# Reading alpha by a 128-partition broadcast transfer, and loading the first x chunk in one transfer, in a scaled-residual kernel

## The chip, the cores and the metric

The kernel runs on one core of a Trainium2 chip. A core has five instruction streams: TensorE (PE), VectorE (DVE), ScalarE (ACT), GpSimd (POOL) and SyncE (SP), and sixteen DMA engines that move data between the device memory (HBM) and the on-chip memory (SBUF, 128 partitions). A transfer is issued by an instruction of one stream and is then carried out by the DMA engines beside it.

The metric is the device time of one execution in microseconds (us), lower is better. Three runs of the kernel before gave 162.13, 162.22 and 162.7 us, with a median of 162.22 us.

## The reference

```python
B, S, D = 512, 32, 640
"x": normal (B, S, D) * 0.05, bfloat16
"fx": normal (B, S, D) * 0.05, bfloat16
"alpha": normal (1,) * 0.05 * 0.1, bfloat16

def reference(x, fx, alpha):
    return x + alpha * fx
```

There are 10,485,760 elements in x, as many in fx, and as many in the output, two bytes each. So 41.94 MB have to be read and 20.97 MB written, with one multiplication and one addition for each element, and one scalar that all of them share.

## The kernel before, in words

x, fx and the output are each seen as 128 rows of 81,920 elements, one row for each partition. The columns are cut into five chunks of 16,384 elements (`CHUNK`, line 13; 32 KB for each partition, 4 MB for the whole chunk). For each chunk k there are a load of x (`load_x`, lines 57 to 60), a load of fx (`load_f`, lines 62 to 64), the computation (`compute`, lines 66 to 77: one VectorE instruction that multiplies fx by the scalar and adds x, and writes over the x tile) and a store of that tile (`store`, lines 79 to 84). The last chunk is computed and stored in two halves.

There are four x buffers (`xs`, line 50) and two fx buffers (`fs`, line 51). All loads and stores of the chunks are issued by SP, in an order written out by hand (lines 86 to 106, `manual_schedule` on line 52): x0, fx0, x1, fx1, x2, then fx2, store 0, x3, fx3, store 1, x4, fx4, store 2, store 3, and the two halves of store 4. The transfers share one DMA queue in that order. A load of fx from chunk 2 on waits for the computation that used its buffer two chunks earlier, the load of x4 waits until store 0 has been written out, and each store waits for its computation. The first load alone, x0, is issued as two transfers: partitions 0 to 15, and then partitions 16 to 127 (line 59). The first moves 0.5 MB and the second 3.5 MB.

The scalar alpha is made available on all partitions ahead of everything else (`alpha_to_lanes`, lines 16 to 27). ACT issues a transfer of the single element to partition 0 (line 20); VectorE fills a row of 128 ones (line 22); TensorE multiplies that row by the element, so that every partition receives it (line 24); and VectorE copies the result into a float32 tile `a_f` (line 26), which all the computations read. On VectorE these two small instructions stand ahead of the first computation.

Of the kernel before, what the change touches and what calls it, by code (L numbers as in the profile page):

```python
# [1 line left out]

# [4 lines left out]

ACT = mybir.ActivationFunctionType
ALU = mybir.AluOpType
F32 = mybir.dt.float32  # L10
BF16 = mybir.dt.bfloat16

CHUNK = 16384


def alpha_to_lanes(nc, consts, psum, alpha, eng):

    P = nc.NUM_PARTITIONS
    a_1 = consts.tile([1, 1], alpha.dtype, name="a_1")
    eng.dma_start(out=a_1[:], in_=alpha[None, :])  # L20
    ones = consts.tile([1, P], alpha.dtype, name="ones")
    nc.vector.memset(ones[:], 1.0)  # L22
    a_ps = psum.tile([P, 1], F32, name="a_ps")
    nc.tensor.matmul(a_ps[:], ones[:], a_1[:], start=True, stop=True)  # L24
    a_f = consts.tile([P, 1], F32, name="a_f")
    nc.vector.tensor_copy(out=a_f[:], in_=a_ps[:])  # L26
    return a_f


@with_exitstack  # L30
def kernel(
    ctx: ExitStack,
    tc: tile.TileContext,
    x: bass.AP,
    fx: bass.AP,
    alpha: bass.AP,
    out: bass.AP,
):
    nc = tc.nc
    P = nc.NUM_PARTITIONS  # L40
    xv = x.flatten_outer_dims().rearrange("(p n) d -> p (n d)", p=P)
    fxv = fx.flatten_outer_dims().rearrange("(p n) d -> p (n d)", p=P)
    ov = out.flatten_outer_dims().rearrange("(p n) d -> p (n d)", p=P)
    F = xv.shape[1]
    K = F // CHUNK
    assert K * CHUNK == F and K == 5

    consts = ctx.enter_context(tc.tile_pool(name="consts", bufs=1))
    psum = ctx.enter_context(tc.tile_pool(name="psum", bufs=1, space=bass.MemoryType.PSUM))
    xs = ctx.enter_context(tc.tile_pool(name="xs", bufs=4))  # L50
    fs = ctx.enter_context(tc.tile_pool(name="fs", bufs=2))
    ctx.enter_context(tc.manual_schedule())

    a_f = alpha_to_lanes(nc, consts, psum, alpha, nc.scalar)
    xt, ft = {}, {}

    def load_x(k):
        xt[k] = xs.tile([P, CHUNK], x.dtype, tag="x", name="x_t")
        for a, b in [(0, 16), (16, P)] if k == 0 else [(0, P)]:
            nc.sync.dma_start(out=xt[k][a:b, :], in_=xv[a:b, bass.ts(k, CHUNK)])  # L60

    def load_f(k):
        ft[k] = fs.tile([P, CHUNK], fx.dtype, tag="f", name="f_t")
        nc.sync.dma_start(out=ft[k][:], in_=fxv[:, bass.ts(k, CHUNK)])

    def compute(k, parts=1):
        n = CHUNK // parts
        for j in range(parts):
            s = bass.ts(j, n)
            nc.vector.scalar_tensor_tensor(  # L70
                out=xt[k][:, s],
                in0=ft[k][:, s],
                scalar=a_f[:],
                in1=xt[k][:, s],
                op0=ALU.mult,
                op1=ALU.add,
            )

    def store(k, j=0, parts=1):
        n = CHUNK // parts  # L80
        nc.sync.dma_start(
            out=ov[:, k * CHUNK + j * n : k * CHUNK + (j + 1) * n],
            in_=xt[k][:, bass.ts(j, n)],
        )

    load_x(0)
    load_f(0)
    load_x(1)
    load_f(1)
    load_x(2)  # L90
    compute(0)
    load_f(2)
    store(0)
    load_x(3)
    compute(1)
    load_f(3)
    store(1)
    load_x(4)
    compute(2)
    load_f(4)  # L100
    store(2)
    compute(3)
    store(3)
    compute(4, 2)
    store(4, 0, 2)
    store(4, 1, 2)


# [1 line left out]
_INS = ['x', 'fx', 'alpha']  # L110
_OUTS = [((512, 32, 640), 'bfloat16')]


# [23 lines left out]
```

## Time and profile before

| | us |
|---|---|
| median of three runs | 162.22 |
| the profiled execution: its own time | 162.22 |
| the profiled execution: span from its first to its last instruction | 160.4 |
| VectorE busy | 86.9 |
| of that, the six computations | 86.6 |
| TensorE busy | 0.2 |
| VectorE's waits for a load of fx, five in all | 59.1 |

The profile is of one execution. A page of it gives for each engine its busy time; the span cut into 40 equal slices, with the share of the DMA engines that was busy and the rate at which they moved data; the DMA queues; the chain of work that ended last, followed back from the end; the costliest groups of instructions with what they waited for; and the transfers, with the time from issue to landing, which is when the completion was signalled. The trace behind the page can be asked for any stretch of time, counted from the start of the span. In a view by stretches the rate counts the bytes of a packet at the packet's start. A packet of these transfers is one partition's row of 32 KB (16 KB in the last two stores).

### The profile page before, as it was taken

How to read it: one execution, taken by the hardware profiler on the slowest of the kernel's cores; microseconds unless marked ns; L12 is line 12 of the kernel's file. 1: busy time of each engine (PE TensorE's matmuls, PEld its weight loads, DVE VectorE, ACT ScalarE, POOL GpSimd, SP SyncE). 2: the span in 40 equal slices, each digit the busy share in tenths (PEclk: the TensorE clock that was granted, in tenths of full speed). 3: DMA queues.
4: the chain of work that ended last, by engine and by line, in shares of the span. 5: the costliest groups of instructions: out<-in, count | busy, mean ns of one | idle time of the engine just before them, and what ended most of it. 6: DMA issues, size and time to landing. Idle time of an engine off the chain costs nothing.

```text
span 160.4 us, 88 instructions
## 1 busy us (share of the span) xinstructions
PE 0.2 (0%) x1; PEld 0.1 (0%) x1; DVE 86.9 (54%) x8; POOL 0.2 (0%) x4
## 2 busy tenths in 40 slices
PE   0000000000000000000000000000000000000000
PEld 0000000000000000000000000000000000000000
DVE  0000000099994999949999000999930049998000
POOL 0000000000000000000000000000000000000000
DMA  9799999999999999999999999999999999999991
GB/s 131 139 261 286 253 351 441 449 417 425 449 433 400 457 441 400 441 466 400 433 449 425 425 449 417 408 449 441 417 417 474 392 417 466 417 425 425 400 445 53
DMA packets 2322, 62.92 MB, mean 392 GB/s; under 512 B 274, under 2 KB 274, under 8 KB 274
## 3 DMA queue, kind: packets, MB, share of 16 engines
q1 hardware_dynamic: 2320, 62.92, 97.1%
q10 hardware_dynamic: 2, 0.00, 0.0%
HBM read 41.94 MB, written 20.97 MB: 392 GB/s over the span
## 4 chain that ended last, share of the span: by engine, by line
DMA 59%; DVE 27%; DVEq 5%; SPq 0%; issue 0%
DMA f_t<-in_fx_dram 59%; DVE x_t L70 27%; DVEq L132 5%; SPq L60 0%; DVEq L70 0%
## 5 line engine op out<-in xcount | busy, mean ns | idle before, releaser
L70 DVE SCALAR_TENSOR_TENSOR x_t<-f_t,a_f,x_t 128x16384 bf16<-128x16384 bf16 (+1 forms) x6 | 86.6, 14439 | 59.1 <-DMA f_t<-in_fx_dram 59.1
L26 DVE COPY a_f<-a_ps 128x1 f32<-128x1 f32 x1 | 0.2, 159 | 1.2 <-PE a_ps L24 1.2
L22 DVE MEMSET ones<- 1x128 bf16 x1 | 0.2, 165 | 0.8 <-PEq L121 0.8
L24 PE MATMUL a_ps<-a,ones 1*128 1x1 bf16 x1 | 0.2, 158 | 1.9 <-DMA a<-in_alpha_dram 1.9
L121 POOL MEMSET const-bfloat16-1.0<- 128x1 bf16 x1 | 0.1, 101 | 0.0
L121 POOL MEMSET const-uint8-127<- 128x1 uint8 x1 | 0.1, 101 | 0.0
L121 POOL MEMSET const-float32-0.0<- 128x1 f32 x1 | 0.1, 98 | 0.2 <-issue 0.2
L121 POOL MEMSET const-float32-1.0<- 128x1 f32 x1 | 0.1, 98 | 0.0
L24 PEld LDWEIGHTS <-ones 1*128 1x128 bf16 x1 | 0.1, 97 | 1.0 <-DVE ones L22 1.0
## 6 DMA issues: line engine op xcount, KB each, us to landing
f_t<-in_fx_dram SPq DMA_DIRECT2D x5, 4096.0 KB, 31.3
x_t<-in_x_dram SPq DMA_DIRECT2D x4, 4096.0 KB, 39.8
out_dram<-x_t SPq DMA_DIRECT2D x4, 4096.0 KB, 40.7
out_dram<-x_t SPq DMA_DIRECT2D x2, 2048.0 KB, 11.5
x_t<-in_x_dram SPq DMA_DIRECT2D x1, 3584.0 KB, 21.3
x_t<-in_x_dram SPq DMA_DIRECT2D x1, 512.0 KB, 7.2
a<-in_alpha_dram ACTq DMA_DIRECT2D x1, 0.0 KB
```

Of the source, the lines that this page charges most:

```text
L22: nc.vector.memset(ones[:], 1.0)
L24: nc.tensor.matmul(a_ps[:], ones[:], a_1[:], start=True, stop=True)
L26: nc.vector.tensor_copy(out=a_f[:], in_=a_ps[:])
L70: nc.vector.scalar_tensor_tensor(out=xt[k][:, s], in0=ft[k][:, s], scalar=a_f[:], in1=xt[k][:, s], op0=ALU.mult, op1=ALU.add,)
L121: nc = _bacc.Bacc("TRN2", target_bir_lowering=False, num_devices=1)
L132: with _tile.TileContext(nc) as tc:
```

## The change

The scalar's path loses the ones, the matmul and the PSUM tile. ACT issues instead one transfer whose source is the single element repeated 128 times and whose destination is one bf16 element on each of the 128 partitions. VectorE's copy to float32 stays; it reads that tile in place of the PSUM tile, and so waits for the transfer in place of the matmul. The first load of x is issued as one transfer of 128 partitions, as the other loads are. Nothing else differs: buffers, order and computations are the same.

```diff
-def alpha_to_lanes(nc, consts, psum, alpha, eng):
+def alpha_to_lanes(nc, consts, alpha, eng):
     P = nc.NUM_PARTITIONS
-    a_1 = consts.tile([1, 1], alpha.dtype, name="a_1")
-    eng.dma_start(out=a_1[:], in_=alpha[None, :])
-    ones = consts.tile([1, P], alpha.dtype, name="ones")
-    nc.vector.memset(ones[:], 1.0)
-    a_ps = psum.tile([P, 1], F32, name="a_ps")
-    nc.tensor.matmul(a_ps[:], ones[:], a_1[:], start=True, stop=True)
+    a_b = consts.tile([P, 1], alpha.dtype, name="a_b")
+    eng.dma_start(out=a_b[:], in_=alpha.to_broadcast((P, 1)))
     a_f = consts.tile([P, 1], F32, name="a_f")
-    nc.vector.tensor_copy(out=a_f[:], in_=a_ps[:])
+    nc.vector.tensor_copy(out=a_f[:], in_=a_b[:])
     return a_f
...
-    psum = ctx.enter_context(tc.tile_pool(name="psum", bufs=1, space=bass.MemoryType.PSUM))
...
-    a_f = alpha_to_lanes(nc, consts, psum, alpha, nc.scalar)
+    a_f = alpha_to_lanes(nc, consts, alpha, nc.scalar)
...
-        for a, b in [(0, 16), (16, P)] if k == 0 else [(0, P)]:
-            nc.sync.dma_start(out=xt[k][a:b, :], in_=xv[a:b, bass.ts(k, CHUNK)])
+        nc.sync.dma_start(out=xt[k][:], in_=xv[:, bass.ts(k, CHUNK)])
```

## The prediction

> **What bounds the kernel now.** I read the slices of the page first, because 62.92 MB in 160.4 us makes the transfers the first suspect.
>
> ```profile
> span 160.4 us, 88 instructions
> ...
> DVE  0000000099994999949999000999930049998000
> ...
> DMA  9799999999999999999999999999999999999991
> GB/s 131 139 261 286 253 351 441 449 417 425 449 433 400 457 441 400 441 466 400 433 449 425 425 449 417 408 449 441 417 417 474 392 417 466 417 425 425 400 445 53
> ```
>
> The DMA engines are busy in every slice but the last, and VectorE has long gaps, so the stream of transfers is the bound. The line below is the one to look at: a slice is 4.0 us, and in the first five or so the busy engines move only 131 to 286 GB/s, in all later ones 392 or more. Busy engines at 60% of the rate are being held up by something. The second view is the list of issues with the time from issue to landing.
>
> ```profile
> x_t<-in_x_dram SPq DMA_DIRECT2D x1, 3584.0 KB, 21.3
> x_t<-in_x_dram SPq DMA_DIRECT2D x1, 512.0 KB, 7.2
> ```
>
> From the timeline and the chain (next fences), SP starts these at 0.73 us (the 16 partitions) and 1.17 us (the 112). So the first piece lands at 0.73 + 7.2 = 7.9 us and the second at 1.17 + 21.3 = 22.5 us. The chain that ended last says when fx0 landed and what followed:
>
> ```profile
> 0.73 0.39 SPq L60
> 1.12 0.06 issue
> 1.17 0.41 SPq L60
> 1.58 0.05 issue
> 1.63 30.55 DMA f_t<-in_fx_dram
> 32.18 0.03 issue
> ```
>
> fx0 lands at 1.63 + 30.55 = 32.18, which is 9.7 us after x0's second piece, although both are about 4 MB. Third, the rate in stretches of 2 us (columns: stretch, its length, busy time of PE, PEld, DVE, POOL, clock, DMA share, GB/s):
>
> ```profile
> 18.00:20.00 2.00, 0.00 (x0) 0.00 (x0) 0.00 (x0) 0.00 (x0) 1.00 1.01 262
> 20.00:22.00 2.00, 0.00 (x0) 0.00 (x0) 0.00 (x0) 0.00 (x0) 1.00 0.84 279
> 22.00:24.00 2.00, 0.00 (x0) 0.00 (x0) 0.00 (x0) 0.00 (x0) 1.00 0.99 426
> 24.00:26.00 2.00, 0.00 (x0) 0.00 (x0) 0.00 (x0) 0.00 (x0) 1.00 1.10 475
> ```
>
> The rate steps up at 22 us, exactly where the second piece ends and the first 128-partition transfer takes over; it does not climb towards it (it is 246 to 295 from 8 us to 22 us). By stages:
>
> ```profile
> 22.50:32.20 9.70, 0.00 (x0) 0.00 (x0) 0.00 (x0) 0.00 (x0) 1.00 1.00 432
> 32.20:51.60 19.40, 0.00 (x0) 0.00 (x0) 17.29 (x1) 0.00 (x0) 1.00 1.00 432
> 51.60:71.00 19.40, 0.00 (x0) 0.00 (x0) 17.28 (x1) 0.00 (x0) 1.00 1.00 432
> ```
>
> A 4.194 MB transfer of 128 partitions at 432 GB/s takes 9.71 us, as fx0 did after x0. Last, the start of VectorE's and PE's work in the timeline:
>
> ```profile
> 0.73 0.50 ACTq L20 DMA_DIRECT2D a<-in_alpha_dram  x1
> ...
> 1.93 0.16 PE L24 MATMUL a_ps<-a,ones 1*128 1x1 bf16 x1 [1.93 <-DMA a<-in_alpha_dram]
> ...
> 2.13 0.16 DVE L26 COPY a_f<-a_ps 128x1 f32<-128x1 f32 x1 [1.15 <-PE a_ps L24]
> ...
> 32.31 17.29 DVE L70 SCALAR_TENSOR_TENSOR x_t<-f_t,a_f,x_t 128x16384 bf16<-128x16384 bf16 x1 [30.02 <-DMA f_t<-in_fx_dram]
> ```
>
> alpha is ready at 2.13 + 0.16 = 2.29 us and first read at 32.31: 30 us early.
>
> **The change part by part. x0 in one transfer.** The DMA view of the first 3 us counts its first bytes in the slice that begins at 1.725 us: the first rows start at about 1.75. So x0 occupies the stream from 1.75 to 22.5, 20.7 us, of which 9.71 are what a transfer of its size takes elsewhere. Issued in the form of the other loads, x0 and fx0 together need 2 x 9.71 = 19.42 us, and fx0 lands at about 1.75 + 19.42 = 21.2, plus two things. In the same view the 16 engines' first rows start spread from 1.725 to 2.475 (the slices with bytes), so the last engine adds up to 0.75; and signalling the landing adds something under 0.9 (the last bytes of the program start in the slice that ends at 158.6, a 16 KB row takes about 0.6, and the span ends at 160.4 with closing work behind it). I take 1.0 for both together: 22.2. Before it was 32.18, so 10.0 us less. Lower end of the gain: 9.2, with both additions full and some lag between the engines that isn't from x0. Upper end: 10.9, with nothing added.
>
> Does the gain reach the end? Behind fx0 the stream never pauses (a share of 1.00 at 428 to 432 GB/s in the stages up to 130.5), so everything rests on the issues coming early enough, and they are released by things that shift along. Computation 0 starts when fx0 lands and ends 17.3 us later, 49.6 before and about 39.6 after. It releases fx2, store 0 and x3. At that time x1, fx1 and x2 are still in the stream, until 22.2 + 3 x 9.71 = 51.3, so 11.7 us of work are queued when fx2 is issued, as before. x4 waits for store 0 to land (10.8 us of SP's waiting), fx3 for computation 1, fx4 for computation 2; each hangs on an earlier landing, and shifts with it. VectorE, 17.3 us per chunk against 29.1 us of transfers (three times 9.71), doesn't become the bound; only at the start does it meet two transfers in 19.4 us, and it then waits 2.12 and 2.13 us for fx1 and fx2, which stays. SP issues one transfer less (0.41 us, line 60), so fx0, x1, fx1 and x2 are issued some 0.45 us earlier, behind a queue that already holds 10 us of work: worth nothing, in either direction.
>
> Two pages of the Trainium skill pull in opposite directions here. "DMA: Bandwidth & Descriptors", Rules for kernel authors, says that transfers to disjoint partition ranges share the same engines and serialize, so that one should use a single transfer; by that alone the split costs about one issue, the sum would be about 0.4 us, and 162 would stay. "SBUF — State Buffer", Door 1, says that the DMA rate depends on how many of 16 ports the partitions reach; by its table partitions 0 to 15 reach four, which would be an estimated 109 GB/s of its 435 for the first piece. The 131 and 139 GB/s in the first two slices agree with the second; for the 112 partitions its table shows no shortage, only engines that could meet on a port, and what it would cost isn't stated there.
>
> **alpha by broadcast.** Removed: a MEMSET (0.17 us), a weight load (0.10), a matmul (0.16), all at 0.8 to 2.1 us, 30 us off the path: worth 0. Added: 128 elements of 2 bytes on the queue of ACT, and DVE's copy now waits for them. Behind that copy on DVE stands computation 0, and for that wait fx2, store 0 and x3 on SP. Cover: the first computation can't start before fx0, 22.2 us. If the elements are shared by the 16 engines as the rows are, eight to each, and each must let one 32 KB row (1.21 us) pass, they land at about 1.2 + 8 x 1.21 + 0.7 = 11.6 us (0.7 from the end of alpha's issue, 1.23, to the matmul's start, 1.93). That leaves 10 us. Nor does lateness cost at once: the stream runs dry at 51.3, so computation 0 may start as late as 51.3 - 17.3 - 0.9 = 33.1 (0.33 for the issue, 0.6 from the first x issue's end to the first row).
>
> What the elements take from the engines themselves: the queue's two packets of before have a share of 0.0% of 16 engines in the first 3 us, below 0.05% of 48 us, or 0.012 us each. Nine on each engine (eight and a signal) would be under 0.11 us. The far row is the 0.7 us above, taken as occupancy eight times over: 5.6 us. I take 0.1, because the first is occupancy and the second is mostly latency; the far end is kept as a rival. A cost below nothing is excluded, since the stream carries only more packets.
>
> **Sum.** -10.0 + 0.1 = -9.9. The profiled execution's own time is 162.22 (span 160.4 and 1.8 around it), the same as the median, so 152.3. By the ends: 162.22 - 10.9 = 151.3 and 162.22 - 9.2 + 0.6 = 153.6 (with a middling 0.6 for alpha's packets). The later stages aren't quite rigid: from the computation that fx2 releases (71.13) to the one that fx4 releases (130.55) are 59.4 us, where six transfers are 58.3, so up to 1 us of chance delay can come or go.
>
> **The rivals.**
>
> *The slowness belongs to the start, not to the split.* The first 20 us of any stream might be slow (the change doesn't do what it says). For: it begins with the first byte. Against: the step at 22 us falls on the boundary of the transfers, and between 8 and 22 us there is no climb. All of it stays: 162.22 + 0.1 = 162.3. A milder form: only the first 0.5 MB is slow by nature. Up to 7.9 us the excess is 6.15 - 0.524/0.432 = 4.9 us at most, so the time would be 157.2.
>
> *alpha starves behind SP's loads (slower).* If the queue of ACT is served only when SP's has nothing, alpha lands after x2, at 51.3. Computation 0 then ends at 68.6, fx2's first row starts 0.9 later at 69.5, and the stream has stood still for 18.2 us: 152.3 + 18.2 = 170.5. It costs from a landing at 33.1 on and eats the whole gain from 43 on. For: x1, fx1 and x2 lie in one queue from 3.6 us. Against: before, alpha was served at once beside x0, issued at the same 0.73.
>
> *alpha's elements occupy the engines.* By the far row 5.6 us: 162.22 - 10.0 + 5.6 = 157.8. Against: the 0.0%.
>
> **How the numbers follow.** Likeliest 0.86 at 152.3, its own range 151.0 to 153.8; start slow by nature 0.03 at 162.3 and 0.04 at 157.2; alpha starved 0.04 at 170.5; alpha's packets 0.03 at 157.8. The likeliest's range with the chance delay of 1 us holds some 0.82 of everything; I give 150.8 to 154.0. Faster by over 0.5% (0.8 us, about what a measurement can tell from no change) are the first, third and fifth: 0.93; same 0.03; slower 0.04.
>
> **What would show it.** Right: slices from the first on at 390 GB/s or more; x0 landing about 10 to 11 us after its issue, fx0 at 22; the first computation at about 22.3, still released by fx0; DVE's copy done before 12 us; the span near 150.5. Wrong: low rates in the first slices again, or a first computation that waits for alpha, or a hole in the DMA share near 50 us.

## The result, and the profile after

The changed kernel takes 153.58 us (median of four runs, 153.41 to 153.82), beside 162.26 us for the kernel before. The ratio is 0.946, with a 95% interval of 0.944 to 0.948: 8.7 us or 5.4% less. The forecast was 152.3 with a range of 150.8 to 154.0, so the sign and the range held and the point was 1.3 us too low. Of the 9.9 us that were forecast, 1.2 did not come, and the experiments below ask where they went.

The profiled execution took 153.67 us, with a span of 151.9. Its page, cut as the page of before was (a slice is now 3.8 us):

```profile
span 151.9 us, 81 instructions
...
DMA  5999999999999999999999999999999999999993
GB/s 173 440 354 362 449 423 423 414 423 440 457 457 423 423 414 414 449 449 440 431 431 423 414 414 431 457 449 423 431 423 423 414 440 449 457 414 397 431 427 160
...
q10 hardware_dynamic: 144, 0.00, 0.0%
```

The long stretch of 131 to 286 GB/s is gone. Two slices, the third and the fourth, are still low (354 and 362). The queue of ACT (q10) now carries 144 packets where it carried 2: 128 elements and 16 signals (a signal is the small packet with which one of the engines reports that its share of a transfer is done). The chain that ended last, at the places that answer to those of before:

```profile
0.73 0.38 SPq L54
1.11 0.05 issue
1.16 23.23 DMA f_t<-in_fx_dram
24.40 0.03 issue
24.42 0.05 DVEq L64
24.47 0.05 issue
24.52 17.30 DVE x_t L64
41.82 0.02 issue
41.84 21.41 DMA f_t<-in_fx_dram
```

fx0 landed at 24.40 us, 7.8 us before its old 32.18, but 2.2 us after the 22.2 that I had worked out. The first computation still follows fx0, and everything behind it has moved along. Alpha became usable much later than forecast, as the timeline of VectorE says:

```profile
15.92 0.15 DVE L22 CAST a_f<-a_b 128x1 f32<-128x1 bf16 x1 [15.92 <-DMA a_b<-in_alpha_dram]
24.52 17.29 DVE L64 SCALAR_TENSOR_TENSOR x_t<-f_t,a_f,x_t 128x16384 bf16<-128x16384 bf16 x1 [8.45 <-DMA f_t<-in_fx_dram]
```

It is there at 15.9 us (forecast 11.6), and 8.45 us of waiting for fx0 still lie between it and its first use. So alpha's lateness cost nothing by itself.

The sum of the two profiled executions closes: 162.22 - 7.78 (fx0 earlier) - 0.77 (the rest of the execution's time, 130.04 before and 129.27 after) = 153.67. What is missing against the forecast is all ahead of fx0, and a little came back behind it: from computation 2 to computation 4 are 58.86 us (63.34 to 122.20) where they were 59.42.

### The profile page after: what moved, and what is told of

It is laid out like the page before. It is cut to its first block, busy times and chain, and to the rows that moved or that the text cites. A ratio compares the mean times of both kernels' runs of the same rounds, so it can differ in the third digit from the quotient of the medians.

```text
span 151.9 us, 81 instructions
## 1 busy us (share of the span) xinstructions
DVE 86.7 (57%) x7; POOL 0.2 (0%) x4
## 4 chain that ended last, share of the span: by engine, by line
DMA 57%; DVE 29%; DVEq 6%; issue 0%; SPq 0%
DMA f_t<-in_fx_dram 57%; DVE x_t L64 29%; DVEq L126 6%; SPq L54 0%; DVEq L64 0%
## 5 line engine op out<-in xcount | busy, mean ns | idle before, releaser
L22 DVE CAST a_f<-a_b 128x1 f32<-128x1 bf16 x1 | 0.2, 154 | 15.9 <-DMA a_b<-in_alpha_dram 15.9
## 6 DMA issues: line engine op xcount, KB each, us to landing
x_t<-in_x_dram SPq DMA_DIRECT2D x5, 4096.0 KB, 38.8
out_dram<-x_t SPq DMA_DIRECT2D x2, 2048.0 KB, 13.4
a_b<-in_alpha_dram ACTq DMA_DIRECT2D x1, 0.2 KB, 15.2
```

The source lines that it names most:

```text
L22: nc.vector.tensor_copy(out=a_f[:], in_=a_b[:])
```

## The experiments

Each time below is a median; the ratio is to the kernel before, measured in the same set of runs (162.4, 162.4 and 162.8 us in the three sets). "fx0" is the time in the span at which the chain has it landed.

**1. The two parts of the change, each alone.** First x0 in one transfer, with alpha's old path:

```diff
-        for a, b in [(0, 16), (16, P)] if k == 0 else [(0, P)]:
-            nc.sync.dma_start(out=xt[k][a:b, :], in_=xv[a:b, bass.ts(k, CHUNK)])
+        nc.sync.dma_start(out=xt[k][:], in_=xv[:, bass.ts(k, CHUNK)])
```

> x0 in one transfer, alpha as before (one element and the ones matmul). Theory A (the 128 elements of alpha, taken between the rows of x0 and fx0, are what made fx0 land at 24.4 us in place of 22.2): fx0 lands at 22.2 to 23.0 and the time is about 1.4 us below the changed kernel's 153.6, so 152.2. Rival R (a stream of 128 partitions starts slowly whatever alpha does): fx0 lands at 24.4 again and the time is 153.6 within 0.3.

Measured: 152.68 us, ratio 0.940 (0.938 to 0.942), span 150.8. The chain of this kernel:

```profile
1.16 21.48 DMA f_t<-in_fx_dram
22.64 0.03 issue
...
40.08 22.34 DMA f_t<-in_fx_dram
62.42 0.03 issue
```

fx0 lands at 22.64, as theory A has it, and the time is 0.9 us below the changed kernel's, with intervals that don't touch. So x0 in one transfer is worth 9.5 us at fx0 (32.18 to 22.64), and the broadcast takes 1.76 of it back (to 24.40). Only half of those 1.76 us show in the time, which is the question of experiment 5.

Then the broadcast alone, with x0 in its two old pieces:

```diff
-        nc.sync.dma_start(out=xt[k][:], in_=xv[:, bass.ts(k, CHUNK)])
+        for a, b in [(0, 16), (16, P)] if k == 0 else [(0, P)]:
+            nc.sync.dma_start(out=xt[k][a:b, :], in_=xv[a:b, bass.ts(k, CHUNK)])
```

(This diff is against the changed kernel.)

> x0 in two transfers as before, alpha by the broadcast. Theory S (the partition ranges of the split are what was slow): the first 22 us stay at 130 to 295 GB/s and the time stays at 162.2; if the elements of alpha cost the stream something there too (theory A), 162.5 to 163.7. Rival (it was alpha's old path that held things up): near 153.6.

Measured: 162.55 us, ratio 1.001 (0.999 to 1.003). The first slices read 130 131 261 261 261 GB/s, as before, and fx0 lands at 32.70, 0.5 us later. Alpha's old path held nothing up, and in a stream that is slow anyway the broadcast can't be told from no change in the time. The two parts don't add up: at fx0 the broadcast's price is 1.76 us without the split and 0.5 with it. The 0.5 itself isn't clear of chance, since fx0 also differs by 0.4 us (22.32 to 22.73) among the kernels of this section that have x0 in 128 partitions and no broadcast.

**2. Is it the split or the partitions?** The same two sizes as the old split, but cut by columns:

```diff
-        for a, b in [(0, 16), (16, P)] if k == 0 else [(0, P)]:
-            nc.sync.dma_start(out=xt[k][a:b, :], in_=xv[a:b, bass.ts(k, CHUNK)])
+        for a, b in [(0, 2048), (2048, CHUNK)] if k == 0 else [(0, CHUNK)]:
+            nc.sync.dma_start(out=xt[k][:, a:b], in_=xv[:, k * CHUNK + a : k * CHUNK + b])
```

> alpha as before; x0 in two transfers again, with the same 0.5 MB and 3.5 MB, but cut by columns (2048 and 14336), each of all 128 partitions. Theory S: no slow phase, fx0 lands within 0.7 us of the kernel with x0 in one transfer, time within 0.5 us of it, 152 to 153. Rival T1 (two transfers in place of one cost the time): 162. Rival T2 (the first 0.5 MB or the first 20 us are slow by nature): the first slices at 130 to 290 GB/s again, 157 to 162.

Measured: 152.60 us, ratio 0.940 (0.937 to 0.942), fx0 at 22.32. The chain's lines for fx0, and the first piece in the list of issues:

```profile
1.64 20.69 DMA f_t<-in_fx_dram
22.32 0.03 issue
...
x_t<-in_x_dram SPq DMA_DIRECT2D x1, 512.0 KB, 3.4
```

Two transfers in place of one cost nothing here, and neither is the first 0.5 MB slow by nature: it landed 3.4 us after its issue, where the 16 partitions of before needed 7.2 for the same bytes.

Then two equal halves by partitions:

```diff
-        for a, b in [(0, 16), (16, P)] if k == 0 else [(0, P)]:
+        for a, b in [(0, 64), (64, P)] if k == 0 else [(0, P)]:
```

> alpha as before; x0 in two transfers of 64 partitions each (0 to 63, 64 to 127). Theory S (the rate depends on which of 16 groups of partitions a transfer reaches, and partitions 0 to 63 reach eight of them): each half moves its 2.1 MB at about half of 432 GB/s, 9.7 us, x0 takes about 19.4 us and the time is near 161. Rival S2 (only a very small or an uneven number of partitions is slow): as with x0 whole, 152.7 within 0.5.

Measured: 163.69 us, ratio 1.008 (1.005 to 1.011), slower even than the old split and 2.7 us above what theory S expected. The rates by stretches of this kernel, with the columns as before (the GB/s last):

```profile
2.00:13.70 11.70, 0.06 (x1) 0.00 (x0) 0.16 (x1) 0.00 (x0) 1.00 1.06 224
13.70:24.10 10.40, 0.00 (x0) 0.00 (x0) 0.00 (x0) 0.00 (x0) 1.00 0.98 230
24.10:33.60 9.50, 0.00 (x0) 0.00 (x0) 0.00 (x0) 0.00 (x0) 1.00 0.99 428
```

While the two halves are loaded, the stream moves at about half of the 428 GB/s at which fx0 follows, with the DMA engines as busy as ever. The stretches end where the halves land, at 13.7 and 24.2 us; engines that are done early have begun the next transfer by then, so that x0 as a whole takes 22 us in place of the expected 19.4. It isn't the smallness of the piece: 2.1 MB in 64 partitions suffer as 0.5 MB in 16 do. The Trainium skill's "SBUF — State Buffer", Door 1, puts partitions 0 to 63 on eight of 16 ports, an estimated 218 GB/s of its 435; the 224 and 230 are near it. The same skill's rule in "DMA: Bandwidth & Descriptors" (Rules for kernel authors) calls a split into partition halves merely useless; here it cost 11 us (fx0 at 33.6 against 22.6).

Two things stay open. The second piece of the old split, 112 partitions at 246 to 295 GB/s, lost more than the first (14.6 us between the two landings, where its 3.67 MB at 432 GB/s are 8.5), and no run has it by itself: the runs show that the cut by partitions is what slows it, and not how. And a transfer of some of the partitions also reads only the rows of x that belong to them, so no run separates the part of the device memory that is read from the part of SBUF that is written.

**3. No alpha at all**, to see the stream's start by itself (against the changed kernel):

```diff
-    a_b = consts.tile([P, 1], alpha.dtype, name="a_b")
-    eng.dma_start(out=a_b[:], in_=alpha.to_broadcast((P, 1)))
     a_f = consts.tile([P, 1], F32, name="a_f")
-    nc.vector.tensor_copy(out=a_f[:], in_=a_b[:])
+    nc.vector.memset(a_f[:], 0.005)
```

> x0 in one transfer and no load of alpha at all: a_f is filled with a constant, so the kernel leaves out alpha. It shows the start of the stream by itself. Theory A: the same as with x0 whole and the one-element alpha, within 0.3 us, about 152.2, fx0 at 22.2 to 23.0. Rival R: 153.6, fx0 at 24.4.

Measured: 152.90 us, ratio 0.941 (0.938 to 0.944), fx0 at 22.68. It equals x0 whole with the one-element alpha: the old path of alpha costs nothing, and 22.6 is what a stream of 128 partitions gives.

**4. What in the broadcast costs 1.8 us?** First, it was put ahead of x0 on the same queue (this diff and the next are against the changed kernel):

```diff
-    a_f = alpha_to_lanes(nc, consts, alpha, nc.scalar)
+    a_f = alpha_to_lanes(nc, consts, alpha, nc.sync)
```

> The changed kernel with alpha's broadcast issued by SP ahead of x0, on the queue of the rows. If the cost of the broadcast is that its elements are taken one by one between rows, they now all go before the first row: alpha lands near 3 us, fx0 at about 23.2 (22.7 with the one-element alpha, plus one more issue ahead, 0.4, and 0.1 for the elements), time 152.7 to 153.2. If the elements occupy the engines wherever they stand: fx0 at 24.4 and 153.6.

Measured: 153.08 us, ratio 0.945 (0.940 to 0.950); alpha lands 3.2 us after its issue, and fx0 at 23.93, between the two expectations. Of the 1.3 us above 22.64, 0.6 are the later issue of x0 (1.33 in place of 0.73). The remaining 0.7 us are less than the 1.76, so the place of the elements matters, but it is not all of it.

Then the broadcast was issued twice:

```diff
+    a_d = consts.tile([P, 1], alpha.dtype, name="a_d")
+    eng.dma_start(out=a_d[:], in_=alpha.to_broadcast((P, 1)))
     eng.dma_start(out=a_b[:], in_=alpha.to_broadcast((P, 1)))
```

> The changed kernel with the broadcast issued twice on the queue of ACT, the second one into the tile that is used. If each element slows the row beside it: fx0 lands 1.0 to 1.8 us later than in the changed kernel, at 25.4 to 26.2, alpha after about 25 to 28 us, so that the first computation may wait for alpha; time 154.5 to 155.5. If the cost is a fixed one of having a second queue open: fx0 at 24.4, 153.6.

Measured: 153.25 us, ratio 0.947 (0.942 to 0.952). My expectation missed: fx0 landed at 24.15 us (1.16 + 23.0) and not at 25.4 to 26.2. Alpha came only at 26.6 and the first computation did wait for it, but x1, by whose landing all elements of both broadcasts had been moved, landed at 33.9, no later than in the changed kernel (34.1), and the time is the same. The 2 us by which computation 0 was late cost nothing, as the forecast's rule on the drying stream had it. Why 256 elements cost no more than 128 stays open.

Last, the number of small packets was kept and their address was changed. Three kernels have x0 whole and the one-element alpha, and beside it a transfer on ACT's queue that only an unused copy on VectorE reads. In the first the 128 elements come from 128 rows of x, in the second all from one element of x, in the third 512 bytes for each partition from one place. The diff leaves out the change of x0; its two comment lines stand for what the second and the third kernel have in place of the transfer above them:

```diff
     a_f = alpha_to_lanes(nc, consts, psum, alpha, nc.scalar)
+    probe = consts.tile([P, 1], x.dtype, name="probe")
+    nc.scalar.dma_start(out=probe[:], in_=xv[:, 0:1])
+    # second: in_=xv[0:1, 0:1].to_broadcast((P, 1))
+    # third:  probe of [P, 256], in_=xv[0:1, 0:256].to_broadcast((P, 256))
+    probe_f = consts.tile([P, 1], F32, name="probe_f")
+    nc.vector.tensor_copy(out=probe_f[:], in_=probe[:, 0:1])
```

> x0 whole and the one-element alpha with the matmul, and beside it a transfer on the queue of ACT that nothing of the result needs: 128 elements of 2 bytes, one from each of 128 different rows of x. If 128 small packets cost the 1.7 us: fx0 at 24.4, time about 153.6, as in the changed kernel. If it is that all of them read one address: fx0 at 22.7 and 152.7.

> As the run with a transfer of 128 elements from 128 rows of x (x0 whole, one-element alpha), but all 128 elements are now read from one element of x. Theory H (128 small reads cost nothing; 128 reads of one address cost): fx0 lands near 24.4 us in place of 22.7, time 153.1 to 153.6. Rival (it is something else about the changed kernel's alpha, such as its tensor or the missing PE work): fx0 at 22.7, 152.6.

> The same with 512 bytes in place of 2 on each partition, all 128 reads from the same 512 bytes of x. Theory H: as late as with 2 bytes, fx0 at 24.4 or a little later (64 KB more are 0.15 us at 432 GB/s). Rival (the cost is that of pieces of 2 bytes from one address): fx0 at 22.7 to 22.9.

The line of the chain that has fx0's load (its start and its length, which together give the landing), for 128 addresses:

```profile
1.16 21.56 DMA f_t<-in_fx_dram
22.73 0.03 issue
```

for one address:

```profile
1.16 23.01 DMA f_t<-in_fx_dram
24.18 0.03 issue
```

and for 512 bytes from one address:

```profile
1.16 22.92 DMA f_t<-in_fx_dram
24.09 0.03 issue
```

128 small packets from different addresses cost 0.1 us, as I had put it. The same packets from one address cost 1.5, and 1.4 with 512 bytes, so their size hardly matters. Each landing is from one execution, but the two groups lie well apart: 22.3 to 22.7 us in the five kernels with x0 in 128 partitions and no reads of one address, 24.1 to 24.4 in the four with such reads on ACT's queue. All of these reads were issued as a repeated source, so the runs don't tell whether it is the address itself or that form of transfer. In the time it is 152.59, 153.50 and 153.34 us, with ratios 0.943 (0.937 to 0.949), 0.943 (0.940 to 0.945) and 0.944 (0.940 to 0.947): a difference of that size is too small for these intervals, so it is the landings that carry the verdict. The DMA view of 4 to 14 us shows it as well. First the changed kernel, then the one with 128 addresses (packets, MB, share of 16 engines):

```profile
q1 hardware_dynamic: 128, 3.67, 92.4%
q10 hardware_dynamic: 125, 0.00, 0.6%
```

```profile
q1 hardware_dynamic: 146, 4.26, 98.9%
q10 hardware_dynamic: 128, 0.00, 0.7%
```

The small packets themselves take the same 0.6 to 0.7% in both, about 8 ns each (0.6% of 160 us, divided by 125). What differs is the rows. In each view 16 of q1's packets are signals, so 112 rows start in 10 us in place of 130 (3.67 and 4.26 MB at 32 KB). In the changed kernel the engines stand without any packet for 7% of the time, and a row takes longer while it moves: 1.32 us (92.4% of 160 us over 112 rows) in place of 1.22. How reads of one address do both stays open.

**5. Where did half of the 1.76 us go?** In the chain of experiment 1, fx2 lands 39.8 us after fx0 (62.42 and 22.64); in the changed kernel 38.9 (63.25 and 24.40). So x0 whole loses 0.9 us again before fx2. The rates say where, first in that kernel:

```profile
54.00:58.00 4.00, 0.00 (x0) 0.00 (x0) 4.00 (x1) 0.00 (x0) 1.00 0.91 393
58.00:62.00 4.00, 0.00 (x0) 0.00 (x0) 1.45 (x1) 0.00 (x0) 1.00 1.12 369
```

Those are the last rows of fx2, ahead of the first store of the run. The order of the two was then changed:

```diff
-    load_f(2)
     store(0)
+    load_f(2)
```

> x0 whole and one-element alpha, with store 0 issued ahead of fx2 in place of behind it. It asks for the 0.9 us that the stream lost later, while the last rows of fx2 moved (58 to 62 us), in all kernels in which fx0 landed before 24. If the loss belongs to the change from fx2's loads to store 0's writes, it goes elsewhere or goes away with the new order, and the time is 151.7 to 152.2. If it belongs to that time of the run, or to what SP issues when computation 1 ends (59.4), rows are slow at 58 to 62 us again and the time stays at 152.7.

Measured: 152.46 us, between the two expectations; the ratio, 0.937 (0.935 to 0.938), just overlaps with the 0.938 to 0.942 of x0 whole. The stretches of this kernel:

```profile
48.00:52.00 4.00, 0.00 (x0) 0.00 (x0) 4.00 (x1) 0.00 (x0) 1.00 0.96 287
52.00:54.00 2.00, 0.00 (x0) 0.00 (x0) 2.00 (x1) 0.00 (x0) 1.00 1.10 475
54.00:58.00 4.00, 0.00 (x0) 0.00 (x0) 4.00 (x1) 0.00 (x0) 1.00 0.95 410
58.00:62.00 4.00, 0.00 (x0) 0.00 (x0) 1.49 (x1) 0.00 (x0) 1.00 1.08 467
```

The slow stretch has moved to 48 to 52 us, one transfer earlier, together with store 0. So it belongs to the hand-over from loads to the first store and not to a moment of the run, and the new order doesn't remove it. The changed kernel shows no such stretch (401 GB/s from 58 to 62 and 492 from 62 to 64). Among the kernels with the old order, those with fx0 at 22.3 to 22.7 us all have it: their fx2 lands 39.5 to 40.1 us after fx0. In all others, with fx0 at 23.9 or later, it lands 38.7 to 39.0 us after, and four transfers of 9.71 are 38.8. What makes the difference stays open.

## Why the prediction was right, and where it missed

*What bounds the kernel, and what the split cost.* Right. The step in the rate at 22 us was the boundary of the transfers, and the slowness went with the partition ranges: columns cost nothing, halves cost 11 us. "I take 1.0 for both together: 22.2" was nearly right: with alpha out of the way fx0 landed at 22.64, so the two additions came to 1.5 and the term was -9.5 in place of -10.0. It lay within its ends. Two readings on the way were loose. The sixth slice, across the boundary of the transfers, reads 351 GB/s and not 392 or more. And the 131 GB/s of the first slice are only the 16 rows that start in it, divided by 4 us; a rate for the 16 partitions comes from the rows' durations, 124.3% of 16 engines for 3 us over 16 rows, or 3.7 us a row where 1.21 is usual.

*Does the gain reach the end.* Right. The releases shifted with fx0, the issues stayed far ahead, and the waits for fx1 and fx2 are 2.11 and 2.14 us as they were 2.12 and 2.13. From fx0 to the end the time changed by 0.8 us, within the "up to 1 us of chance delay".

*alpha's cover.* Right in the verdict, though the landing was at 15.9 and not at 11.6. The 128 elements from 128 addresses, which held nothing up, landed 14.2 us after their issue, where these took 15.2, so most of the lateness is waiting beside the rows, which "8 x 1.21" sized too low. The broadcast issued twice showed a part of the margin: computation 0 at 26.81 instead of 24.52 cost nothing.

*alpha's packets.* This is the step that failed: "Nine on each engine (eight and a signal) would be under 0.11 us ... I take 0.1". The occupancy was sized rightly, 8 ns a packet. But I took occupancy for the whole price, and the row of before that I took it from was one element read by one engine; 128 reads of one address, which no row of before showed, held the rows beside them up by 1.76 us at fx0. In the time this is 0.9 us, since the kernel with x0 whole and the old path of alpha loses 0.9 us of its lead where its first store begins. The far end that I kept, 5.6 us, was too large by a factor of three.

*The sum.* At fx0 the forecast missed by 2.1 us: 0.46 from x0 and 1.66 from the broadcast (1.76 in place of 0.1). The late stages gave 0.8 back, against a forecast of none, and the median stands 0.1 below the profiled execution. That is the 1.3 us. So the point came this close in part by luck: the 0.8 us of the late stages was no term of the sum, and it covered a good third of the miss.

*The signs of being right.* The first computation followed fx0, and the low stretch was gone. Four signs, though, did not come: slices from the first on at 390 GB/s or more (173, 354 and 362), x0 10 to 11 us after its issue (13.4), DVE's copy before 12 us (15.9) and a span near 150.5 (151.9).

*The rivals.* A slow start by nature is refuted by the column split and by the kernel without alpha. alpha starved behind SP's loads didn't happen: its elements went out between the rows. The rival of alpha's elements holding up the engines is the one that came true in small, by rows that were delayed and not by the elements' own time.

## What to carry to other kernels

A load that reaches only part of the partitions can run at a fraction of the rate while all DMA engines look busy, so look for a rate that steps up where one transfer ends and another begins; if a load has to be cut, cut it by columns. A one-element broadcast by DMA is not free beside a saturated stream although its packets are tiny: here 128 reads of one address delayed the rows where 128 reads of different addresses did not. Where one element and a matmul are off the path, they are the cheaper way. x0 whole or cut by columns, with the old path of alpha, beats both kernels: 152.7 and 152.6 us.

## What I had not expected of the hardware

Reads of one address, 128 of them beside the rows, delayed large transfers on the same engines by 1.4 to 1.8 us in all, with 2 bytes as with 512, whereas reads of 128 addresses delayed them by 0.1. A second such broadcast right behind the first cost nothing more. And the last two rows of each engine's load ahead of the first store ran slowly in some of the kernels (287 to 385 GB/s for 4 us, 0.7 to 1.2 us lost), at a place that moved when the store was moved.
